# One-lane steps with 56 moving columns, and attention outputs evicted by halves

## The chip, the cores and the metric

The kernel runs on 1 core of one Trainium2 chip. The metric is the time of one execution on the device in microseconds (us). Before the change it is 3534.4 us, the median of 3 runs (3536.71, 3530.97 and 3534.40 us).

Five engines appear in the profile. PE is TensorE's stream of matmuls and PEld the weight loads in front of them, DVE is VectorE, ACT is ScalarE, POOL is GpSimd, and SP (SyncE) issues nearly all DMAs here. Matmul results land in PSUM; DVE and ACT move them on into SBUF, here called an eviction.

## The reference

Four layers stand one behind the other: a recurrent attention block A, an MLP block B, and both again with the same weights. All tensors are bf16.

```python
def _A_ref(x, mem0, Wq, Wk, Wv, Wo, seg_len):     # S 2048, Dm 640, H 32 heads, Dh 192, M 8, seg 32
    L = M + seg_len                                # 40
    mask = (idx[:, None] < M) | (idx[:, None] >= idx[None, :])
    mem = mem0
    for s in range(n_seg):                         # 64 segments, in sequence
        h = jnp.concatenate([mem, xs], axis=1)     # 40 rows: 8 of memory, 32 of the segment
        q = jnp.einsum('btd,dhe->bhte', h, Wq)     # and k, v alike
        scores = jnp.where(mask, q @ k.T * scale, -1e9)
        o = softmax(scores) @ v
        o = jnp.einsum('bhte,hed->btd', o, Wo)
        mem = o[:, :M, :]                          # the next segment's memory
        outs.append(o[:, M:, :])

x = x + _A_ref(_layernorm(x), A_mem0, ...)
x = x + _B_ref(_layernorm(x), ...)                 # layernorm, w1, gelu, shifts, w2, layernorm, w3, gelu, w4
x = x + _A_ref(_layernorm(x), A_mem0, ...)
x = x + _B_ref(_layernorm(x), ...)
```

The memory makes the 64 segments of one A a chain: a segment starts when the first 8 output rows of the one before it are there.

## The kernel before

**Steps and lanes.** The two A blocks run interleaved as two lanes. Lane 0 is the first A at segment `t`, lane 1 the second A at segment `t - LAG` with `LAG = 5`. `attention_step(t)` is called for `t` from 0 to 68. In steps 5 to 63 both lanes are there, and their rows stand side by side in one tile: the transposed input `hT` has 5 chunks of 128 partitions by `NS = 80` columns, lane 0 in columns 0 to 39 and lane 1 in 40 to 79. In steps 0 to 4 only lane 0 runs and in steps 64 to 68 only lane 1: `N` is then `L1 = 40` and `c0` (0 or 40) is the first column of the lane that runs. These ten are the one-lane steps. Every second step from t = 2 on also carries a chunk of block B (`chunk`, `chunk_end`), 64 rows of each lane; the last chunk runs alone behind step 68, the tail.

**One step.** The 32 heads go in 8 groups of 4, the groups in 4 pairs. For each pair `proj_pair` makes k, q and v, transposed: six output chunks of 128 by five contraction chunks, so 30 matmuls per group and kind, 720 in a step (L541). The weights are stationary and `hT` moves, so every matmul has a weight load of its own and moves 80 columns, or 40 in a one-lane step. q and v leave PSUM through ACT (L551, L571), k through DVE (L559, L565). v is transposed on PE (L579) and evicted in halves: ACT takes one (L590), DVE the other (L588). `attend` makes the scores (L606), the masked row minimum on DVE (L617), exp on ACT (L624), the sum and the scaling on DVE (L628 to L630), a transpose (L639) that leaves through ACT (L644), and P·V (L653). Its result `pso`, 128 partitions by 6 chunks by 80 columns in f32, leaves through one DVE cast (L659) into one of 8 buffers `oT`. The output projection takes 6 by 5 matmuls per group, 240 in a step (L670), into `psy`. All groups but the first have it due at the end of the step. `fm` (L688, ACT) then copies the 8 memory rows to the next step's `hT`, and `fy` (L696, DVE) hands the other rows to block B.

**Weights.** SBUF holds part of the weights. The rest is streamed again in every step by SP, in blocks of 384 KB through a ring of 8 buffers (L453), and block B's weights through a ring of 3 (L486 to L494). In step 0 the resident weights come in too.

**Order.** Each operation is added to a `Plan` with its engine, a length, a due time and the buffers it reads and writes. `place()` makes one list of them all by simulating the engines, the PSUM slots and the DMA rate; the program is written out in that order, so each engine works through a fixed queue. A DMA that the plan held back for its rate (`paced`) gets a wait for the PE operation that had ended by then in the plan. PSUM is 8 slots of one bank: 6 in class A, 2 in class B. Where two engines read one PSUM tile, the build puts a semaphore between them in the order in which the plan wrote them; the plan's own times do not hold that wait.

Planned lengths of matmul groups come from

```python
def mm_us(n, m=128, k=1):
    return k * (max(54, n) / 2400.0 + 0.0025)
```

Of the kernel before, what the change touches and what calls it, by code (L numbers as in the profile page):

```python
# [29 lines left out]
OT_BUFS = 8  # L30
LAT = 0.12
# [44 lines left out]
class Plan:  # L76
# [47 lines left out]
    def place(self):  # L124
# [27 lines left out]
        def est(o, t):  # L152
            s = max(t, o.ready)
            need = {}
            for b in o.slots:
                if b.slot is None:
                    need[b.cls] = need.get(b.cls, 0) + 1
            for c, n in need.items():
                fs = self.free_slots[c]
                if len(fs) < n:  # L160
                    return None
                s = max(s, fs[n - 1][0])
            if o.e == "SP":
                s = max(s, srv - ahead(o))
            return s
# [6 lines left out]
        while left:  # L172
            best = None
            for e in engines:
                t = free[e]
                lst = cand[e]
                if not lst:
                    continue
                vals = []
                m = None  # L180
                for o in lst:
                    s = est(o, t)
                    if s is not None:
                        vals.append((s, o))
                        if m is None or s < m:
                            m = s
                if m is None:
                    continue
                if best is not None and m >= best[0]:
                    continue  # L190
                lim = m + (0.12 if e == "PE" else 0.05)
                s, o = min((so for so in vals if so[0] <= lim), key=lambda so: (so[1].due, so[1].i))
                if best is None or s < best[0]:
                    best = (s, o)
            assert best is not None, "no operation can be placed"
            s, o = best
            e = o.e
            for b in o.slots:
                if b.slot is None:
                    b.slot = self.free_slots[b.cls].pop(0)[1]  # L200
            o.start = s
            o.paced = e == "SP" and s <= srv - ahead(o) + 1e-9
            o.end = s + o.d
            free[e] = o.end
            done = o.end
            if o.dma:
                srv = max(s + DMA_FIRST, srv) + o.dma / (DMA_START if o.due < STEP else DMA_RATE)
                done = srv + DMA_LAST + o.margin
            cand[e].remove(o)
            out.append(o)  # L210
            left -= 1
            for b in o.slots:
                b.left -= 1
                b.free_at = max(b.free_at, done + LAT)
                if b.left == 0:
                    heapq.heappush(self.free_slots[b.cls], (b.free_at, b.slot))
                    self.free_slots[b.cls].sort()
            for x in o.succ:
                if o.dma:
                    at = done  # L220
                elif x.e == e:
                    at = o.end
                else:
                    at = o.end + (PE_LAT if e == "PE" else LAT)
                if at > x.ready:
                    x.ready = at
                x.n -= 1
                if x.n == 0:
                    offer(x)
            if o.i in in_queue:  # L230
                q, k = in_queue[o.i]
                head[q] = k + 1
                lst = self.queues[q]
                if k + 1 < len(lst) and lst[k + 1].i in waiting:
                    x = waiting.pop(lst[k + 1].i)
                    cand[x.e].append(x)
# [4 lines left out]
def kernel(  # L241
# [87 lines left out]
    mask_b = ctile([L1, L1], bf16, "mask_b")  # L329
    nc.gpsimd.memset(mask_b[:], 0.0)  # L330
    keep(mask_b, L1, M, L1, -M, 1, -1, NEG)
    keep(mask_b, L1, M, L1, -M, 1, 0, 0.0)
# [11 lines left out]
    qT = qTw[:].rearrange("p (c n) -> p c n", c=GC)  # L344
    vFw = ctile([P, GC * NS], bf16, "vF")
    vF = vFw[:].rearrange("p (c n) -> p c n", c=GC)
    kT = [ctile([P, 8, NS], bf16, f"kT{i}") for i in range(2)]
    Vt = [ctile([NS, 2 * VP], bf16, f"V{i}") for i in range(2)]
# [23 lines left out]
    for i in range(2):  # L372
        nc.gpsimd.memset(kT[i][:], 0.0)
    for i in range(2):
        nc.vector.memset(Vt[i][:], 0.0)
    nc.gpsimd.memset(yTB[:], 0.0)
    nc.vector.memset(qTw[:], 0.0)
    nc.vector.memset(vFw[:], 0.0)
    nc.vector.memset(Pmw[:], 0.0)
# [131 lines left out]
    def attention_step(t):  # L511
# [4 lines left out]
        maskt = mask2[:] if both else (mask_a if 0 in ln else mask_b[:])  # L516
# [8 lines left out]
        def proj_pair(pr):  # L525
            s0 = base + sl * 2 * pr
            for kind, off in (("k", 0.0), ("q", 0.2), ("v", 0.5)):
                wbs, wv = load_pair(kind, pr, s0 + off * 2 * sl, LEAD_A)
                for j in range(2):
                    g = 2 * pr + j  # L530
                    G = t * NG + g
                    due = s0 + (off + 0.1 * j) * 2 * sl
# [3 lines left out]
                    for kcs in [range(0, nres)] + [range(kc, kc + 1) for kc in range(nres, KC)]:  # L536
                        def fn(op, pq=pq, wv=wv, j=j, kcs=kcs):
                            o = T(pq)
                            for cc in range(GC):
                                for kc in kcs:  # L540
                                    nc.tensor.matmul(out=o[:, cc, 0:N],  # L541
                                                     lhsT=wv(kc, GW * j + cc * P, GW * j + (cc + 1) * P),
                                                     rhs=h[:, kc, c0:c0 + N], start=(kc == 0 and cc == 0),
                                                     stop=(kc == KC - 1), skip_group_check=True)
                        wb = wbs[0] if kcs[0] == 0 else wbs[1 + kcs[0] - nres]
                        add("PE", mm_us(N, k=GC * len(kcs)), due + 0.01 * kcs[0], fn, r=(wb, *hk), a=(pq,))
                    if kind == "q":
                        q = qT

                        def fq(op, pq=pq, q=q):  # L550
                            nc.scalar.copy(out=q[:, :, 0:N], in_=T(pq)[:, :, 0:N])  # L551
                        add("ACT", act_us(GC * N), due, fq, r=(pq,), w=(B("qT"),))
                    elif kind == "k":
                        k_ = kT[G % 2]

                        def fk(op, pq=pq, k_=k_):
                            p4 = T(pq)[:].rearrange("p (h c) n -> p h c n", h=2)
                            k4 = k_[:].rearrange("p (h c) n -> p h c n", h=2)
                            nc.vector.tensor_copy(out=k4[:, :, 0::3, 0:N], in_=p4[:, :, 0::2, 0:N])  # L559
                        add("DVE", dve_us(4 * N), due, fk, r=(pq,), w=(B("kT", G % 2, 0),))  # L560
                        for part, (r0, r1, jj) in enumerate(((0, 64, 1), (64, P, 2))):
                            def fk2(op, pq=pq, k_=k_, r0=r0, r1=r1, jj=jj):
                                p4 = T(pq)[:].rearrange("p (h c) n -> p h c n", h=2)
                                k4 = k_[:].rearrange("p (h c) n -> p h c n", h=2)
                                nc.vector.tensor_copy(out=k4[r0:r1, :, jj, 0:N], in_=p4[r0:r1, :, 1, 0:N])  # L565
                            add("DVE", dve_us(2 * N), due, fk2, r=(pq,), w=(B("kT", G % 2, 1 + part),))
                    else:
                        vf, V_ = vF, Vt[G % 2]

                        def fvf(op, pq=pq, vf=vf):  # L570
                            nc.scalar.copy(out=vf[:, :, 0:N], in_=T(pq)[:, :, 0:N])  # L571
# [3 lines left out]
                        def fvt(op, pvt=pvt, vf=vf):  # L575
# [6 lines left out]
                        for hf in range(2):  # L582
                            def fe(op, pvt=pvt, V_=V_, hf=hf):
                                src = T(pvt)[0:N, GWH * hf:GWH * (hf + 1)].rearrange("n (a b) -> n a b", a=2)
                                v0 = hf * (VP - 64)
                                dst = V_[0:N, v0:v0 + 512].rearrange("n (a b) -> n a b", a=2)[:, :, 64 * hf:64 * hf + Dh]
# [5 lines left out]
                                w=(B("V", G % 2, hf),))  # L592

        def attend(g):
            G = t * NG + g
            s0 = base + sl * g
            q, k_, V_ = qT, kT[G % 2], Vt[G % 2]
# [3 lines left out]
            def fs(op):  # L601
                o = T(pss)
                seq = [(0, 1, 0, 0), (1, 1, 2, 3), (2, 1, 3, 4), (3, 1, 5, 7), (0, 2, 1, 1), (2, 2, 4, 5)]
                for n_, (i, w_, c, j) in enumerate(seq):
                    m_ = wide(c, GC - 1)
                    nc.tensor.matmul(out=o[0:m_, i * N:(i + w_) * N].rearrange("p (a b) -> p a b", a=w_),  # L606
                                     lhsT=qTw[:, c * NS:c * NS + m_], rhs=k_[:, j:j + w_, 0:N],
                                     start=(n_ == 0), stop=(n_ == len(seq) - 1), skip_group_check=True)
            add("PE", mm_us(N, N, 4) + mm_us(2 * N, N, 2), hi - 4, fs,
                r=(B("qT"), B("kT", G % 2, 0), B("kT", G % 2, 1), B("kT", G % 2, 2)), w=(pss,))  # L610
# [4 lines left out]
            def f1(op):  # L615
                o = T(pss)[0:N, 0:HG * N].rearrange("p (a b) -> p a b", a=HG)
                nc.vector.tensor_tensor_reduce(out=o, in0=o, in1=maskt.unsqueeze(1).to_broadcast([N, HG, N]),  # L617
                                               scale=-scale, scalar=3.0e38, op0=ALU.add, op1=ALU.min,
                                               accum_out=sm_[0:N, 0:1])
            add("DVE", dve_us(HG * N) + 0.02, hi - 4, f1, r=(pss,), w=(pss, smk))  # L620

            def f2(op):
                o = T(pss)[0:N, 0:HG * N].rearrange("p (a b) -> p a b", a=HG)
                nc.scalar.activation(out=Pb[0:N, :, 0:N], in_=o, func=ACT.Exp, bias=sm_[0:N, 0:1], scale=-1.0)  # L624
            add("ACT", act_us(HG * N) + 0.09, hi - 4, f2, r=(pss, smk), w=(Pk,))

            def f3(op):
                nc.vector.tensor_reduce(out=sm_[0:N, 2:2 + HG], in_=Pb[0:N, :, 0:N], axis=AX.X, op=ALU.add)  # L628
                nc.vector.reciprocal(out=sm_[0:N, 6:6 + HG], in_=sm_[0:N, 2:2 + HG])
                nc.vector.tensor_tensor(out=Pb[0:N, :, 0:N], in0=Pb[0:N, :, 0:N],  # L630
                                        in1=sm_[0:N, 6:6 + HG].unsqueeze(2).to_broadcast([N, HG, N]), op=ALU.mult)
# [11 lines left out]
            def f5(op):  # L643
                nc.scalar.copy(out=Pt[:, :, 0:N], in_=T(pst)[0:NS, :, 0:N])  # L644
# [10 lines left out]
            add("PE", mm_us(N, k=8), hi - 3, f6, r=(B("PT"), B("V", G % 2, 0), B("V", G % 2, 1)), w=(pso,))  # L655
            o_ = oT[G % OT_BUFS]

            def f7(op):
                nc.vector.tensor_copy(out=o_[:, :, 0:N], in_=T(pso)[:, :, 0:N])  # L659
            add("DVE", dve_us(GC * N), hi - 4, f7, r=(pso,), w=(B("oT", G % OT_BUFS),))  # L660
            due = base + STEP - 1 + 0.02 * g if g >= NG - OT_BUFS + 1 else s0 + 2.0 * sl
            wb, wo = res_tile(("o", g), [P, GC, Dm], Wo_v[:, g], base + STEP - 2 + 0.02 * g)
            for hf in range(2):
                def f8(op, hf=hf):
                    o = T(psy)
                    for cc in range(3 * hf, 3 * hf + 3):
                        for m in range(KC):
                            st = first_wo[0]
                            first_wo[0] = False
                            nc.tensor.matmul(out=o[:, m, c0:c0 + N], lhsT=wo[:, cc, m * P:(m + 1) * P],  # L670
                                             rhs=o_[:, cc, 0:N], start=st, stop=True, skip_group_check=True)
                add("PE", mm_us(N, k=3 * KC), due, f8, r=(wb, B("oT", G % OT_BUFS)), a=(psy,))

# [487 lines left out]
```

## Time and profile before

| what | value |
|---|---|
| median of the runs shown | 3534.4 us |
| profiled execution, own time | 3528.87 us |
| its span, first to last instruction | 3527.2 us |
| step 0 (weights come in) | 0 to 88.3 us |
| steps 1 to 4, one lane | 88.3 to 282.6 us |
| steps 5 to 63, two lanes | 282.6 to 3245.4 us |
| steps 64 to 68, one lane | 3245.4 to 3482.9 us |
| tail, the last chunk of block B | 3482.9 to 3527.2 us |
| DVE busy, ACT busy | 2469.2 us (70%), 1520.6 us (43%) |
| DMA | 1075.27 MB, mean 305 GB/s |
| mean granted TensorE clock | 0.980 |

The bounds of the steps are the ends of each step's last L670 matmuls, where `fy` starts. Busy PE time is the union of the single matmuls' spans. One matmul is in the pipeline for some 200 ns while the next starts 25 to 36 ns behind it, so a busy PE says little of its rate; that is read from the distance of starts. "issue" as releaser of a wait means that the profile shows nothing that the engine waited for.

### The profile page before, as it was taken

Reading aid. Unit: us, or ns where it says so; the run is one execution under the profiler, and the core shown is the slowest. Engines: PE = TensorE matmul, PEld = TensorE weight load, DVE = VectorE, ACT = ScalarE, POOL = GpSimd, SP = SyncE. Lnnn points to the kernel's source line nnn. Section 1 sums busy time; section 2 is a strip of 40 time slices with the busy share of each in tenths; the row PEclk is TensorE's granted clock in tenths of the full one; section 3 lists DMA queues with packets and bytes.
Section 4 is the critical chain, followed back from the end, with each engine's and each line's share of the span. In section 5 each row is a group of like instructions: output and inputs, shape, how many; then the busy total and the mean of one; then the engine's idle time right before and its main releaser. Section 6 shows DMA issues by size and latency. Waiting matters only on the chain.

```text
span 3527.2 us, 188048 instructions
## 1 busy us (share of the span) xinstructions
PE 3322.3 (94%) x84559; PEld 3231.6 (92%) x84559; DVE 2469.2 (70%) x7436; ACT 1520.6 (43%) x3569; POOL 247.1 (7%) x488
## 2 busy tenths in 40 slices
PE   5889999999999999999999999999999999999886
PEld 5879999999999999999999999999999999999775
DVE  2557777777777777777777777777777777777554
ACT  1334444444444444444444444444444444444332
POOL 0000000000000000000000000000000000000000
PEclk8899999999999999999999999999999999999897
DMA  9999898889888988898889888998889888988995
GB/s 374 304 306 317 301 324 298 294 297 316 301 307 299 315 300 299 309 321 303 302 301 327 306 295 298 316 310 303 312 305 319 298 299 301 319 300 303 307 315 176
DMA packets 497753, 1075.27 MB, mean 305 GB/s; under 512 B 49455, under 2 KB 216893, under 8 KB 496945
## 3 DMA queue, kind: packets, MB, share of 16 engines
q1 hardware_dynamic: 489712, 1050.11, 86.2%
q8 instruction: 661, 10.83, 1.2%
q0 software_dynamic: 7232, 13.13, 1.1%
q14 instruction: 148, 1.20, 0.1%
HBM read 1057.79 MB, written 5.24 MB: 301 GB/s over the span
## 4 chain that ended last, share of the span: by engine, by line
PE 88%; DMA 5%; issue 4%; DVE 1%; ACT 1%; SPq 1%; POOL 0%; POOLq 0%; DVEq 0%; ACTq 0%
PE psy L670 16%; PE psq L541 15%; PE psv L541 15%; PE psk L541 15%; PE pvt L579 5%; PE pso L653 4%; PE pss L606 4%; PE psh L998 3%; PE y L1024 3%; PE pst L639 2%; DMA wst<-in_A_Wq_dram 2%; PE psh L918 1%; DMA wst<-in_A_Wk_dram 1%; PE hs L963 1%; DMA wst<-in_A_Wv_dram 1%
## 5 line engine op out<-in xcount | busy, mean ns | idle before, releaser
L541 PEld LDWEIGHTS <-wst 128*128 128x128 bf16 x25668 | 1031.2, 100 | 43.1 <-issue 25.0
L670 PE MATMUL psy<-oT,wo 128*128 128x80 bf16 (+1 forms) x16560 | 689.8, 199 | 32.1 <-issue 19.4
L670 PEld LDWEIGHTS <-wo 128*128 128x128 bf16 x16560 | 626.3, 100 | 41.0 <-issue 29.2
L551 ACT CAST qT<-psq 128x480 bf16<-128x480 f32 (+1 forms) x552 | 292.6, 530 | 639.9 <-PE psq L541 638.6
L541 PE MATMUL psq<-hT,wst 128*128 128x80 bf16 (+1 forms) x9936 | 467.9, 199 | 19.1 <-issue 11.1
L659 DVE CAST oT<-pso 128x480 bf16<-128x480 f32 (+1 forms) x552 | 341.2, 618 | 167.2 <-PE pso L653 161.6
L541 PE MATMUL psv<-hT,wv 128*128 128x80 bf16 (+1 forms) x9936 | 434.6, 199 | 21.1 <-issue 15.9
L541 PE MATMUL psk<-hT,wst 128*128 128x80 bf16 (+1 forms) x9108 | 428.0, 199 | 11.0 <-issue 7.9
L541 PEld LDWEIGHTS <-wv 128*128 128x128 bf16 x9936 | 386.6, 100 | 28.9 <-issue 18.3
L644 ACT COPY PT<-pst 80x320 bf16<-80x320 bf16 (+1 forms) x552 | 221.9, 402 | 440.2 <-PE pst L639 433.8
L590 ACT COPY V<-pvt 80x384 bf16<-80x384 bf16 (+1 forms) x552 | 261.7, 474 | 328.5 <-PE pvt L579 301.1
L541 PE MATMUL psk<-hT,wk 128*128 128x80 bf16 (+1 forms) x7452 | 348.8, 199 | 19.5 <-ACT hT L688 10.8
L565 DVE CAST kT<-psk 64x160 bf16<-64x160 f32 (+1 forms) x1104 | 336.7, 305 | 9.7
L624 ACT ACTIVATE Pm<-pss,sm 80x320 bf16<-80x320 f32 (+1 forms) x552 | 279.7, 507 | 135.9 <-DVE sm L617 135.8
L571 ACT CAST vF<-psv 128x480 bf16<-128x480 f32 (+1 forms) x552 | 290.0, 525 | 102.0 <-PE psv L541 95.7
L541 PE MATMUL psq<-hT,wq 128*128 128x80 bf16 (+1 forms) x6624 | 320.2, 199 | 11.7 <-issue 6.6
L541 PE MATMUL psv<-hT,wst 128*128 128x80 bf16 (+1 forms) x6624 | 322.4, 199 | 7.7 <-issue 6.6
L541 PEld LDWEIGHTS <-wk 128*128 128x128 bf16 x7452 | 299.2, 100 | 26.8 <-issue 26.1
L588 DVE COPY V<-pvt 80x384 bf16<-80x384 bf16 (+1 forms) x552 | 188.1, 350 | 182.3 <-PE pvt L579 107.8
L617 DVE CUSTOM_DVE_ANT_1 pss<-pss,mask 80x320 f32<-80x320 f32 (+1 forms) x512 | 240.9, 485 | 104.7 <-PE pss L606 84.3
L559 DVE CAST kT<-psk 128x320 bf16<-128x320 f32 (+1 forms) x552 | 254.6, 461 | 69.6 <-PE psk L541 63.2
L628 DVE TENSOR_REDUCE sm<-Pm 80x4 f32<-80x320 bf16 (+1 forms) x552 | 248.9, 451 | 57.3 <-ACT Pm L624 52.2
(130 smaller groups left out, 4425.0 us busy)
## 6 DMA issues: line engine op xcount, KB each, us to landing
wst<-in_A_Wq_dram SPq DMA_DIRECT2D x828, 384.0 KB, 5.3
wst<-in_A_Wk_dram SPq DMA_DIRECT2D x759, 384.0 KB, 5.3
wst<-in_A_Wv_dram SPq DMA_DIRECT2D x552, 384.0 KB, 5.4
wstB<-in_B_w_dram SPq DMA_DIRECT2D x495, 320.0 KB, 5.0
wstB<-in_B_w_dram SPq DMA_DIRECT2D x132, 160.0 KB, 4.9
wo<-in_A_Wo_dram SPq DMA_DIRECT2D x8, 960.0 KB, 12.8
wv<-in_A_Wv_dram SPq DMA_DIRECT2D x4, 1152.0 KB, 11.9
wq<-in_A_Wq_dram SPq DMA_DIRECT2D x4, 768.0 KB, 11.7
```

The lines of the kernel that those rows point to most:

```text
L541: nc.tensor.matmul(out=o[:, cc, 0:N], lhsT=wv(kc, GW * j + cc * P, GW * j + (cc + 1) * P), rhs=h[:, kc, c0:c0 + N], start=(kc == 0 and cc ...
L551: nc.scalar.copy(out=q[:, :, 0:N], in_=T(pq)[:, :, 0:N])
L559: nc.vector.tensor_copy(out=k4[:, :, 0::3, 0:N], in_=p4[:, :, 0::2, 0:N])
L565: nc.vector.tensor_copy(out=k4[r0:r1, :, jj, 0:N], in_=p4[r0:r1, :, 1, 0:N])
L571: nc.scalar.copy(out=vf[:, :, 0:N], in_=T(pq)[:, :, 0:N])
L590: nc.scalar.copy(out=dst, in_=src)
L617: nc.vector.tensor_tensor_reduce(out=o, in0=o, in1=maskt.unsqueeze(1).to_broadcast([N, HG, N]), scale=-scale, scalar=3.0e38, op0=ALU.add, ...
L624: nc.scalar.activation(out=Pb[0:N, :, 0:N], in_=o, func=ACT.Exp, bias=sm_[0:N, 0:1], scale=-1.0)
L628: nc.vector.tensor_reduce(out=sm_[0:N, 2:2 + HG], in_=Pb[0:N, :, 0:N], axis=AX.X, op=ALU.add)
L644: nc.scalar.copy(out=Pt[:, :, 0:N], in_=T(pst)[0:NS, :, 0:N])
L659: nc.vector.tensor_copy(out=o_[:, :, 0:N], in_=T(pso)[:, :, 0:N])
L670: nc.tensor.matmul(out=o[:, m, c0:c0 + N], lhsT=wo[:, cc, m * P:(m + 1) * P], rhs=o_[:, cc, 0:N], start=st, stop=True, skip_group_check=True)
```

## The change

It has four parts.

1. **Columns.** In a one-lane step the dense projections (q, k, v) and the output projection move `W = 56` columns, of which the 40 of the running lane are kept. The window is columns 0 to 55 for lane 0 (`cw = 0`, `off = 0`) and 24 to 79 for lane 1 (`cw = 24`, `off = 16`). The evictions copy 40 columns. Tiles that only lane 1 fills keep its rows in columns 40 to 79, so that the softmax of its steps runs over 80 partitions instead of 40 (`NR`), with the same number of elements in each.
2. **Halves.** The cast of `pso` (L659) becomes two in every group of every step: chunks 0 to 2 through DVE, chunks 3 to 5 through ACT, both from the same PSUM bank. Each half has its own dependency, and the three output chunks of the projection that read it wait for that half alone.
3. **Setup.** The eight `oT` are set to zero on POOL and the four `hT` on DVE. `mask_b` is now a slice of `mask2`, and its own three small POOL operations go.
4. **Plan.** `paced` is set in `est` where the rate alone held the DMA back. New names (`KT_BUFS`, `VT_BUFS`) stand for numbers that stay as they were.

```diff
+HALVES = tuple(range(8))
+ONE = 56
...
             if o.e == "SP":
+                s0 = s
                 s = max(s, srv - ahead(o))
+                o.paced = s > s0 + 1e-9
...
-            o.paced = e == "SP" and s <= srv - ahead(o) + 1e-9
...
-    mask_b = ctile([L1, L1], bf16, "mask_b")
-    nc.gpsimd.memset(mask_b[:], 0.0)
-    keep(mask_b, L1, M, L1, -M, 1, -1, NEG)
-    keep(mask_b, L1, M, L1, -M, 1, 0, 0.0)
+    mask_b = mask2[:, L1:NS]
...
+    for o_ in oT:
+        nc.gpsimd.memset(o_[:], 0.0)
...
+    for i in range(4):
+        nc.vector.memset(hT[i][:], 0.0)
...
+        NR = c0 + N
+        W = NS if both else max(ONE, L1)
+        cw = min(c0, NS - W)
+        off = c0 - cw
...
-                                    nc.tensor.matmul(out=o[:, cc, 0:N],
+                                    nc.tensor.matmul(out=o[:, cc, 0:W],
...
-                                                     rhs=h[:, kc, c0:c0 + N], start=(kc == 0 and cc == 0),
+                                                     rhs=h[:, kc, cw:cw + W], start=(kc == 0 and cc == 0),
...
-                        add("PE", mm_us(N, k=GC * len(kcs)), due + 0.01 * kcs[0], fn, r=(wb, *hk), a=(pq,))
+                        add("PE", mm_us(W, k=GC * len(kcs)), due + 0.01 * kcs[0], fn, r=(wb, *hk), a=(pq,))
...
-                            nc.scalar.copy(out=q[:, :, 0:N], in_=T(pq)[:, :, 0:N])
+                            nc.scalar.copy(out=q[:, :, c0:c0 + N], in_=T(pq)[:, :, off:off + N])
...
-            def f7(op):
-                nc.vector.tensor_copy(out=o_[:, :, 0:N], in_=T(pso)[:, :, 0:N])
-            add("DVE", dve_us(GC * N), hi - 4, f7, r=(pso,), w=(B("oT", G % OT_BUFS),))
+            oks = [B("oT", G % OT_BUFS, hf) for hf in range(2)]
+            if g in HALVES:
+                for hf in range(2):
+                    def f7(op, hf=hf):
+                        if hf:
+                            nc.scalar.copy(out=o_[:, 3:6, off:off + N], in_=T(pso)[:, 3:6, 0:N])
+                        else:
+                            nc.vector.tensor_copy(out=o_[:, 0:3, off:off + N], in_=T(pso)[:, 0:3, 0:N])
+                    add("ACT" if hf else "DVE", (act_us if hf else dve_us)(3 * N), hi - 4, f7, r=(pso,), w=(oks[hf],))
...
-                            nc.tensor.matmul(out=o[:, m, c0:c0 + N], lhsT=wo[:, cc, m * P:(m + 1) * P],
-                                             rhs=o_[:, cc, 0:N], start=st, stop=True, skip_group_check=True)
-                add("PE", mm_us(N, k=3 * KC), due, f8, r=(wb, B("oT", G % OT_BUFS)), a=(psy,))
+                            nc.tensor.matmul(out=o[:, m, cw:cw + W], lhsT=wo[:, cc, m * P:(m + 1) * P],
+                                             rhs=o_[:, cc, 0:W], start=st, stop=True, skip_group_check=True)
+                add("PE", mm_us(W, k=3 * KC), due, f8, r=(wb, oks[hf]), a=(psy,))
```

Built, the changed program has the same 169,120 PE instructions. Its order on PE is another: cut into runs of matmuls of one kind, the program before has 6978 runs and the changed one 6889, and 5211 of them stand in the same sequence. ACT has 552 instructions more. Of the 552 pairs of halves, the build makes DVE's half wait for ACT's in 413 and ACT's wait for DVE's in 139.

## The prediction

> **What bounds the kernel now.** First the page, for what the whole span is made of.
>
> ```profile
> span 3527.2 us, 188048 instructions
> PE 3322.3 (94%) x84559; PEld 3231.6 (92%) x84559; DVE 2469.2 (70%) x7436; ACT 1520.6 (43%) x3569; POOL 247.1 (7%) x488
> PEclk8899999999999999999999999999999999999897
> q8 instruction: 661, 10.83, 1.2%
> ```
>
> PE is the busiest engine; its granted clock falls below full only at both ends. The q8 queue carries PE's own code: 169,118 matmuls and weight loads over 661 packets are 256 instructions, 128 matmuls, per 16 KB packet. The clock record shows only 1.00 and 0.50 and changes at multiples of 3.41 us. Then busy time by stage, cut at the ends of steps:
>
> ```profile
> 236.10:282.60 46.50, 41.27 (x1250) 39.52 (x1247) 32.19 (x119) 18.46 (x54) 2.57 (x6) 0.92 0.90 306
> 282.60:3245.40 2962.80, 2887.74 (x72353) 2825.08 (x72349) 2182.50 (x6359) 1345.09 (x3064) 212.86 (x411) 1.00 0.89 306
> 3292.70:3343.40 50.70, 41.52 (x1216) 38.80 (x1212) 24.85 (x95) 16.79 (x50) 4.68 (x8) 0.90 0.94 313
> ```
>
> Columns: stretch, length, busy PE, PEld, DVE, ACT, POOL, clock, DMA share, GB/s. One-lane steps last 46 to 51 us, as long as a two-lane step (2962.8 over 59 steps, 50.2), with half the columns and a clock of 0.90. To see why, matmuls in one of them by time (start, length, engine, line, tiles, form, count, wait):
>
> ```profile
> 3262.27 0.35 PE L541 MATMUL psk<-hT,wk 128*128 128x40 bf16 x8
> 3264.55 0.25 PE L541 MATMUL psk<-hT,wk 128*128 128x40 bf16 x4 [1.93 <-issue]
> 3264.66 0.74 PE L541 MATMUL psk<-hT,wst 128*128 128x40 bf16 x18
> 3265.23 0.57 PE L541 MATMUL psk<-hT,wk 128*128 128x40 bf16 x12
> ...
> 3270.18 0.46 PE L541 MATMUL psq<-hT,wq 128*128 128x40 bf16 x12
> 3270.48 0.30 PE L541 MATMUL psq<-hT,wst 128*128 128x40 bf16 x6
> ```
>
> From one start to the next: 12 matmuls in 0.30 us (25 ns) at full clock, 18 in 0.57 us (32 ns) behind the wait. The view by stretches says why: few matmuls at clock 1.00, then a stretch at half.
>
> ```profile
> 3261.30:3264.70 3.40, 1.47 (x52) 1.39 (x49) 2.47 (x11) 1.89 (x6) 0.00 (x0) 1.00 1.03 372
> 3264.70:3268.20 3.50, 3.50 (x95) 3.50 (x93) 1.41 (x5) 0.86 (x3) 0.22 (x1) 0.51 0.76 224
> ```
>
> Counting starts in order, nearly all "issue" waits in steps 64 to 68 fall at one place modulo 128, just behind a q8 packet: PE is out of code. Who waits in steps 64 to 68 (total us, times, longest):
>
> ```profile
> PEld L541 <- issue: 16.8, 15, 2.1
> PEld L670 <- issue: 7.9, 8, 2.0
> PEld L653 <- ACT V L590: 4.9, 7, 1.2
> PEld L639 <- DVE Pm L630: 2.5, 5, 0.9
> ```
>
> I cut steps 1 to 4 and 64 to 68 (428 us in whole blocks) into 84 code blocks of 128 matmuls and split each block's time: its matmuls at full clock, waits for code, other waits over 0.12 us, and the remainder, which is mostly half clock. 41 blocks end in a code wait, 50 us in all; the remainder is 24 us, and there are 24 half-clock windows. The same cut in the two-lane steps gives 2826 us of matmuls in 2942 us, 41 of code waits at the boundaries, and only some 25 us in which PE waits for ACT or DVE (an own sum over all its waits). There PE is the bound.
>
> **The change part by part.** The sum is made against the profiled execution, 3528.9 us (span 3527.2 and 1.7 around it), 5.5 below the median shown; I carry the difference over.
>
> *Columns, their price.* 56 columns are in no row. 40 move in 25 ns, 80 in 36 (in the chain of waits 30 of psq take from 1042.00 to 1043.08 us), 128 in 55 (psh L918, 15 from 3257.21 to 3258.04). The line through the last two gives 36 - 24 x 0.40 = 26.3; the floor is 25. I take 25.8, between the two and nearer the line: 0.8 ns more. Ten steps have 7200 matmuls at L541 and 2400 at L670: 9600 x 0.8 = 7.7 us, bounds 0 and 12.5. Step 0 hides its share: it moves 374 GB/s and PE waits there for DMAs. Blocks that end in a code wait hide theirs in it. At half clock the price is larger: 40 columns 33 ns (12 from 3265.23 to 3265.63), 128 some 100 (L579, 6 from 3266.23 to 3266.83), so 56 some 46 on the line between.
>
> *Columns, the clock.* [...] Each then costs 3.41 x (1 - 26/46) x 0.85 of it filled = 1.26 us, 10 in all, so 14 of 24 us go.
>
> *What is late next.* The next code packet. A block can't end before its packet; in blocks with a code wait PE goes on some 2.3 us after the packet starts. With that floor in every block, removing all half-clock time shortens the 84 blocks by 17.2 us (9.3 early, 7.9 late) with the 0.8 ns already in. For 14 of 24 that is **-10 us**. Bounds: -17 with no half clock left; +17 where every window stays at half clock and its matmuls pay 46 for 33 ns (1700 x 13 = 22, with 3 at full clock, times the 0.7 that the packets let through).
>
> [...]
>
> *Halves.* The rows, with ACT's from the q cast of the same widths:
>
> ```profile
> L659 DVE CAST oT<-pso 128x480 bf16<-128x480 f32 x472 | 308.9, 655 | 138.2 <-PE pso L653 133.0
> L659 DVE CAST oT<-pso 128x240 bf16<-128x240 f32 x80 | 32.3, 403 | 29.1 <-PE pso L653 28.6
> L551 ACT CAST qT<-psq 128x240 bf16<-128x240 f32 x80 | 28.7, 359 | 103.1 <-PE psq L541 102.0
> ```
>
> DVE falls by 472 x 0.252 + 80 x 0.126 = 129 us, ACT rises by 472 x 0.359 + 80 x 0.26 (by the slope of 480 to 240) = 190 us. But both halves read one bank, and the build orders them. The V halves show what that means: of 552 pairs (L590, L588) none overlaps, the second starts 0.03 us behind the first at best. So an eviction takes 0.36 + 0.03 + 0.40 = 0.79 us for 0.655 before, in one-lane steps 0.26 + 0.03 + 0.28 = 0.57 for 0.40. In 413 of 552 DVE stands behind ACT's half, and behind DVE's stand the softmax reduce (L628, next in its queue in 165) and V (98), for which PE waits; behind ACT's stand the q cast (137), PT (78) and V (72). The plan knows nothing of this order. Cover: the output projection is due at the end of the step, and PE waited for oT only 2.9 us in 7 cases. At the end of one-lane steps it is exposed: 0.17 x 9 = 1.5 us. In two-lane steps I take +0.5, **+2 us** together. Bounds: -8 (DVE's relief takes a third of PE's 25 us of waits) and +24 (one PT or V per step late by the other half, 0.40 x 59).
>
> [...]
>
> *Setup.* Eight POOL memsets of 128x480 at 0.58 x 480/640 = 0.44 us (kT's, 128x640, its next starts 0.58 later) less mask_b's 0.5 put 3.0 us ahead of the first L721 on POOL (7.04 us), and so of the first L541 matmul (9.43). The four hT memsets (0.9 us) sit in DVE's 3.02 us wait for POOL. PE then meets the same weights: it waits 1.0 us for wq at 12.6 and 1.8 for wv, which lands at 19.4. SP's ring waits move 3 us, with DMAs issued to 9.8 us still draining. Taken 0; +3 if uncovered.
>
> *Plan.* `paced` says the same but for ties: 0. The new PE order moves which blocks of two-lane code are dense: 0, bounds -8 and +8, a fifth of 41.
>
> Sum: -10 + 2 = -8, so 3521 for the profiled execution; from the median, **3526 us**.
>
> **Rivals.**
> *The clock comes back whole* (3526 - 7 - 6 = 3513): no half clock left (-17) and DVE's relief shows (-4). For it: the early blocks' waits for DVE. [...]
> *The packets eat it* (3535): all that PE gains it waits for code. For it: 41 of 84 blocks. Against: blocks behind a slow window end with no wait.
> *The ordered halves* (slower): 0.40 us per two-lane step, +24 - 10 + 1.5 = 3550. Its point: two-lane steps longer by over 0.14 us (8/59). For it: 413 waits of DVE on ACT, where V's already idle DVE 70.6 us in 103. Against: those cost PE only a few us.
> [...]
>
> **How the numbers follow.** 0.2% is 7 us, about what a measurement tells from no change. Forecast 0.42 (3516 to 3535: faster 0.30, same 0.12); clock whole 0.22, faster; packets 0.14 (same 0.11, faster 0.02, slower 0.01); halves 0.15 and gate 0.07, slower. Faster 0.54, same 0.23, slower 0.23. From the whole clock's 3513 less the 8 of a lucky order, 3505, to the halves' 3550: left out are about half of both slower cases (0.11) and the edge below.
>
> **What would show it.** Mean start distance of 56-column matmuls 25.8 ns; clock in steps 64 to 68 at 0.95 or more, with about half as many half-clock windows; code waits in those steps above 27 us; these steps shorter by some 5 us in all, the four early ones as much; no oT halves that overlap; two-lane steps at 50.2 ± 0.15. Wrong if one-lane steps keep their length, or two-lane steps move more than one-lane ones.

## The result, and the profile after

| kernel | median, us | executions | ratio to before, 95% |
|---|---|---|---|
| before | 3535.56 (3530.97 to 3538.52) | 6 | |
| after | 3532.66 (3524.69 to 3541.13) | 6 | 0.9992 (0.9977 to 1.0008) |
| after, timed again | 3535.20 (3523.68 to 3551.98) | 12 | 0.9996 (0.9978 to 1.0015) |

No change that can be measured. In the second timing the kernel before ran 35 times, median 3533.82, from 3519.64 to 3549.31: single executions of one program lie up to 30 us apart. So the profiled execution after, 4.2 us shorter than the one before, tells nothing by itself; what the profiles can tell is where PE's time goes.

The page after, with the lines shown of before:

```profile
span 3523.0 us, 188714 instructions
PE 3322.2 (94%) x84559; PEld 3230.5 (92%) x84559; DVE 2344.6 (67%) x7440; ACT 1696.1 (48%) x4121; POOL 250.8 (7%) x493
PEclk7999999999999999999999999999999999999998
q8 instruction: 661, 10.83, 1.2%
```

DVE lost 124.6 us and ACT gained 175.5 (forecast 129 and 190), PE's busy time is the same to 0.1 us. Busy time by stage, first after and then before, both cut at the ends of steps 0, 4, 63 and 68 (at the start of `fy`, which puts the bounds of before 0.6 us later than the table ahead of the prediction; columns as in the prediction):

```profile
88.70:281.80 193.10, 162.47 (x4850) 155.10 (x4850) 105.85 (x414) 75.73 (x230) 8.10 (x17) 0.94 0.91 308
281.80:3239.70 2957.90, 2890.78 (x72349) 2825.03 (x72347) 2066.14 (x6360) 1501.90 (x3536) 212.66 (x411) 1.00 0.89 307
3239.70:3479.00 239.30, 198.85 (x6058) 189.78 (x6057) 130.89 (x510) 93.16 (x282) 16.43 (x31) 0.97 0.90 304
```

```profile
88.90:283.20 194.30, 164.21 (x4860) 156.46 (x4860) 109.56 (x415) 67.91 (x198) 8.12 (x17) 0.89 0.91 306
3246.00:3483.50 237.50, 200.32 (x6058) 189.87 (x6057) 134.76 (x511) 83.94 (x242) 15.66 (x31) 0.91 0.91 306
```

The clock in the one-lane steps rose from 0.89 and 0.91 to 0.94 and 0.97, and yet steps 1 to 4 and 64 to 68 take 432 us together, as before. DMA share and rate didn't move either. Matmuls of one of these steps by time:

```profile
3266.84 0.47 PE L551 MATMUL psv<-hT,wst 128*128 128x56 bf16 x12
3267.15 0.60 PE L551 MATMUL psv<-hT,wv 128*128 128x56 bf16 x17
3269.12 0.19 PE L551 MATMUL psv<-hT,wv 128*128 128x56 bf16 x1 [1.38 <-issue]
3269.15 0.47 PE L551 MATMUL psv<-hT,wst 128*128 128x56 bf16 x12
3269.46 0.49 PE L589 MATMUL pvt<-ident,vF 128*128 128x128 bf16 x6
```

Twelve matmuls of 56 columns start over 0.31 us (26 ns each). One matmul short of its 18 the engine stops for lack of code, 1.38 us, and behind the stop it goes on at 26 ns: the granted clock from 3268.8 to 3272.2 us is 1.00, where before a stretch at 32 ns and a clock of 0.51 followed. Who waits in steps 64 to 68 (total us, times, longest):

```profile
DVE oT L675 <- ACT oT L673: 24.3, 22, 2.5
PEld L551 <- issue: 20.9, 20, 2.8
PEld L690 <- issue: 8.4, 11, 1.9
```

The waits for code at the dense projections were 16.8 us in 15 and are 20.9 in 20; the longest went from 2.1 to 2.8.

To add this up I split all of PE's time, from one matmul's start to the next, into the matmuls at full clock, waits over 0.12 us by what released them, and the rest, mostly half clock. A wait that the profile puts down to "issue" is counted as a wait for code: in the two-lane steps before, all 116 of them stand at the boundary of a code block. Half-clock windows are the pieces of 3.41 us that the clock record has at 0.50. This sum is used below for every kernel, in us:

| kernel | nine one-lane steps | matmuls | rest | code | ACT | DVE | half-clock windows |
|---|---|---|---|---|---|---|---|
| before | 431.7 | 318.3 | 24.8 | 51.6 | 19.0 | 17.9 | 24 |
| after | 432.5 | 323.2 | 18.3 | 54.6 | 22.3 | 14.6 | 10 |
| after, again | 433.0 | 323.2 | 14.4 | 59.6 | 22.1 | 14.2 | 8 |

| kernel | two-lane steps 5 to 63 | code | ACT | DVE | DMA |
|---|---|---|---|---|---|
| before | 2962.8 | 71.9 | 20.9 | 4.1 | 11.7 |
| after | 2957.9 | 62.8 | 24.4 | 11.9 | 5.1 |
| after, again | 2971.4 | 69.9 | 24.0 | 11.9 | 8.4 |

In the nine steps 5 us more of matmuls and 6 to 10 less of half clock stand against 3 to 8 more of code waits. In the two-lane steps the changed kernel differs by 13.5 us from one profiled execution to the other.

### The profile page after: what moved, and what is told of

The parts are those of the page before. It is cut to its first block, busy times and chain, and to the rows that moved or that the text cites. A ratio compares the mean times of both kernels' runs of the same rounds, so it can differ in the third digit from the quotient of the medians.

```text
span 3523.0 us, 188714 instructions
## 1 busy us (share of the span) xinstructions
PE 3322.2 (94%) x84559; PEld 3230.5 (92%) x84559; DVE 2344.6 (67%) x7440; ACT 1696.1 (48%) x4121; POOL 250.8 (7%) x493
## 3 DMA queue, kind: packets, MB, share of 16 engines
q8 instruction: 661, 10.83, 1.2%
## 4 chain that ended last, share of the span: by engine, by line
PE 89%; issue 4%; DMA 3%; DVE 2%; ACT 1%; SPq 1%; POOL 0%; POOLq 0%; DVEq 0%; ACTq 0%
PE psy L690 16%; PE psq L551 16%; PE psv L551 16%; PE psk L551 15%; PE pvt L589 5%; PE pso L663 4%; PE pss L616 4%; PE psh L1018 3%; PE y L1044 3%; PE pst L649 2%; PE psh L938 1%; PE hs L983 1%; DMA wst<-in_A_Wq_dram 1%; DMA wst<-in_A_Wv_dram 1%; ACT V L600 1%
## 5 line engine op out<-in xcount | busy, mean ns | idle before, releaser
L551 PE MATMUL psq<-hT,wst 128*128 128x80 bf16 (+1 forms) x9936 | 452.3, 200 | 14.3 <-issue 9.7
L675 DVE CAST oT<-pso 128x240 bf16<-128x240 f32 (+1 forms) x552 | 213.5, 387 | 314.6 <-ACT oT L673 304.8
L600 ACT COPY V<-pvt 80x384 bf16<-80x384 bf16 x552 | 262.1, 475 | 316.8 <-PE pvt L589 298.6
L551 PEld LDWEIGHTS <-wv 128*128 128x128 bf16 x9936 | 386.6, 100 | 20.5 <-issue 14.6
L634 ACT ACTIVATE Pm<-pss,sm 80x320 bf16<-80x320 f32 (+2 forms) x552 | 280.1, 507 | 140.9 <-DVE sm L627 140.9
L627 DVE CUSTOM_DVE_ANT_1 pss<-pss,mask 80x320 f32<-80x320 f32 (+2 forms) x552 | 253.7, 473 | 134.0 <-PE pss L616 120.0
L551 PE MATMUL psq<-hT,wq 128*128 128x80 bf16 (+1 forms) x6624 | 321.2, 200 | 10.3 <-DVE V L598 4.4
L598 DVE COPY V<-pvt 80x384 bf16<-80x384 bf16 x552 | 190.7, 350 | 194.4 <-ACT V L600 119.7
L673 ACT CAST oT<-pso 128x240 bf16<-128x240 f32 (+1 forms) x552 | 190.1, 344 | 267.6 <-PE pso L663 218.4
L638 DVE TENSOR_REDUCE sm<-Pm 80x4 f32<-80x320 bf16 (+2 forms) x552 | 249.4, 452 | 75.9 <-ACT Pm L634 67.0
```

The costliest lines, as they stand in the source:

```text
L551: nc.tensor.matmul(out=o[:, cc, 0:W], lhsT=wv(kc, GW * j + cc * P, GW * j + (cc + 1) * P), rhs=h[:, kc, cw:cw + W], start=(kc == 0 and cc ...
L598: nc.vector.tensor_copy(out=dst, in_=src)
L600: nc.scalar.copy(out=dst, in_=src)
L634: nc.scalar.activation(out=Pb[0:NR, :, c0:c0 + N], in_=o, func=ACT.Exp, bias=sm_[0:NR, 0:1], scale=-1.0)
L638: nc.vector.tensor_reduce(out=sm_[0:NR, 2:2 + HG], in_=Pb[0:NR, :, c0:c0 + N], axis=AX.X, op=ALU.add)
L675: nc.vector.tensor_copy(out=o_[:, 0:3, off:off + N], in_=T(pso)[:, 0:3, 0:N])
```

## The experiments

Theory: in one-lane steps PE can't be faster than its code arrives, and the code arrives behind the weight traffic; so 56 columns buy nothing there. Rivals: the columns do gain, and the halves take it back; or the columns cost what the clock gives.

**The change again, and its two halves undone, alone and together** (35 runs of before on the same chip). `e1_after_again` is the changed kernel as it is.

> The changed kernel itself, timed once more beside its variants. Both theories: 3525 to 3540 us, a ratio to the kernel before of 0.998 to 1.000, steps 1 to 4 and 64 to 68 together 432 us within 3 (431.8 before, 432.5 in the changed kernel's profile).

3535.20 us, 0.9996 (0.9978 to 1.0015): the same.

`e2_cols40` moves 40 columns again; the planned lengths keep 56, so that every queue has the order of the changed kernel.

```diff
+MOVE = 40
...
-        W = NS if both else max(ONE, L1)
+        W = NS if both else max(MOVE, L1)
+        WP = NS if both else max(ONE, L1)
...
-                        add("PE", mm_us(W, k=GC * len(kcs)), due + 0.01 * kcs[0], fn, r=(wb, *hk), a=(pq,))
+                        add("PE", mm_us(WP, k=GC * len(kcs)), due + 0.01 * kcs[0], fn, r=(wb, *hk), a=(pq,))
```

> The changed kernel with 40 moving columns in one-lane steps, planned with the length of 56, so that every queue keeps its order. Theory 'code packets' (the nine one-lane steps 1 to 4 and 64 to 68 are as long as PE's code takes to come in, so a faster clock is spent on waiting for code): the nine steps 432 us within 4, some 22 half-clock windows in them instead of 10, code waits no longer than with 56; time within 0.15% of the changed kernel. Rival 'clock' (the half-clock windows cost what they seem to, some 10 us, and something else in the change took it back): the nine steps 440 us or more and the time some 10 us (0.3%) above the changed kernel.

3536.43 us, 0.9999 (0.9981 to 1.0018). The nine steps took 426.9 us (432 within 4 expected) with 17 half-clock windows (some 22 expected) and 52.8 of code waits: no longer than with 56 columns, and `e5_own_whole` below has 426.2 with 56. The rival's 10 us are not there: what 56 columns give the clock doesn't show in the time.

`e3_whole_cast` puts the whole cast where DVE's half stands, and a copy of one column in place of ACT's half, in the same order:

```diff
-                            nc.scalar.copy(out=o_[:, 3:6, off:off + N], in_=T(pso)[:, 3:6, 0:N])
+                            nc.scalar.copy(out=spare[:, 1:2], in_=spare[:, 0:1])
-                            nc.vector.tensor_copy(out=o_[:, 0:3, off:off + N], in_=T(pso)[:, 0:3, 0:N])
+                            nc.vector.tensor_copy(out=o_[:, :, off:off + N], in_=T(pso)[:, :, 0:N])
```

> The changed kernel with the attention output leaving PSUM whole through VectorE again, in the place of its half; ScalarE copies one element of an unrelated tile in the place of the other half, so that every queue keeps its order and only the pair on one bank is gone. Theory 'no matter' (output projections are late enough): time within 0.2% of the changed kernel, two-lane steps 50.1 us on average within 0.15. Rival 'ordered halves cost' (VectorE stands behind ScalarE's half for 305 us in all and hands on the delay): two-lane steps 0.2 us shorter or more, time 10 us or more below the changed kernel. Rival 'relief' (a VectorE with 130 us more work delays the softmax): 8 us or more above it.

3546.78 us, 1.0033 (1.0014 to 1.0052): the theory by which the cast doesn't matter fails, and so does the rival that the ordered halves cost; the rival "relief" holds in this order. `e4_cols40_whole` is both edits.

> Both undone in the changed kernel's order: 40 columns and the whole cast. What is left of the change is its order of the queues and its setup. Theory: within 0.2% of the kernel before and of the changed one, and the four kernels of this series within 8 us of each other. A rival, that columns and halves each move the time by 8 us or more and cancel: then e2 and e3 lie on opposite sides of the changed kernel and this one beside it.

3544.21 us, 1.0024 (1.0007 to 1.0042): slower than before, though columns and cast are those of before. What is left is the order, with the setup and the one-column copies on ACT. The time lies where the order acts: in `e3_whole_cast` the two-lane steps took 2980.9 us, and PE waited there 24.4 us for DVE, twice as much as after, while its waits for ACT stayed at 24.9 us (24.4 after). From its waits in steps 5 to 63:

```profile
DVE oT L677 <- PE pso L665: 146.8, 127, 3.3
PE psy L692 <- DVE oT L677: 6.1, 31, 0.7
```

Where the order was made for halves, DVE's relief is worth about 12 us (3547 for 3535). The columns again make no difference: 40 and 56 give 3544 and 3547.

**The whole cast in an order of its own.** `e5_own_whole` sets `HALVES = ()`, so that the plan knows of the 480-wide cast; 56 columns stay.

> The changed kernel with the whole cast on VectorE in all groups, planned as such, so that the queues are ordered for it; 56 columns stay. Theory 'the plan had covered it' (e3 was slow because its order was planned for a VectorE with 130 us less to do): two-lane steps 2963 us within 8 as in the kernel before, PE's waits for VectorE in them 4 to 8 us instead of 24, time within 0.2% of the kernel before. Rival 'relief' (VectorE's work itself delays PE whatever the order, by the 17 us between e3 and the mean of e1 and the changed kernel): two-lane steps 2975 us or more, ratio 1.002 or more.

3530.69 us (12 executions; before 3535.20 in 22), 0.9986 (0.9968 to 1.0003), and PE's waits for DVE in two-lane steps 4.4 us, as before the change. The two-lane steps took 2969.3 us, within the 8 us expected. The plan had already laid its order around the long cast; the halves were relief for nothing.

**Where the one-lane steps' time comes from.** `e6_light` takes the traffic away: in steps 1 to 4 and 64 to 68 each streamed block brings 128 of its 1536 columns, and the projections read resident weights instead (the numbers computed there are other ones, in all else the same instructions).

```diff
+                n = 128 if few else PW
-                nc.sync.dma_start(out=T(b)[:, 0:PW], in_=w_src[kind][:, kc, cols])
+                nc.sync.dma_start(out=T(b)[:, 0:n], in_=w_src[kind][:, kc, PW * pr:PW * pr + n])
+            if few:
+                kc = kc % nres
```

> The changed kernel; in steps 1 to 4 and 64 to 68 the projections take resident weights in place of the streamed ones, of which each DMA brings only 128 of 1536 columns (so the output is not the reference's). Every queue keeps its order and PE its instructions; those steps move some 11 MB less each. Theory 'code packets behind weight traffic': the packets come sooner, code waits in the nine steps fall from 55 us to under 15, the steps from 432 us to 395 or less. Rival 'chain' (the softmax hand-overs through VectorE and ScalarE set the length): code waits fall, waits for VectorE and ScalarE take their place, the steps stay above 420. Rival 'code alone' (packets are slow by themselves): nothing changes.

One execution, 3480.56 us. Its stages 1 to 4 and 64 to 68, its two largest waits for code in steps 64 to 68, and its DMA queues there (packets, MB, share of 16 engines):

```profile
89.00:255.50 166.50, 154.36 (x4847) 148.76 (x4847) 105.41 (x414) 75.17 (x230) 8.11 (x17) 0.98 0.36 96
3230.20:3435.40 205.20, 190.43 (x6058) 183.22 (x6057) 130.21 (x511) 92.95 (x282) 16.42 (x31) 1.00 0.36 95
```

```profile
PEld L693 <- issue: 3.5, 7, 0.7
PEld L554 <- issue: 2.4, 7, 0.5
```

```profile
q1 hardware_dynamic: 32947, 18.25, 33.8%
q8 instruction: 46, 0.75, 1.6%
```

The same queues after, over the same steps:

```profile
q1 hardware_dynamic: 33292, 71.34, 87.9%
q8 instruction: 47, 0.77, 1.3%
```

The same code in almost the same number of packets, a quarter of the weights: the nine steps fall from 432 to 371.7 us, waits for code from 55 to 1.2, half-clock windows from 10 to 2. By the packet records a packet of code in steps 64 to 68 starts on average 0.84 us after PE began the block before it, against 2.23.

`e7_light40` is the same with 40 columns.

> The same with 40 moving columns. Theory: with the packets early, PE's own pace counts, half clock comes less often too (fewer code waits to trigger it), and 40 columns save their 6 us of matmuls against whatever half clock is left: nine steps within 8 us of e6. If half clock was the limit behind the packets: more half-clock windows than in e6 and steps longer by 8 us or more.

One execution, 3474.01 us; the nine steps 371.9 us, against 371.7. So even where code is no limit, 56 columns only balance: 5.3 us more of matmuls, 2.7 less of rest (7 half-clock windows become 2) and 2.3 less of code waits. As far as one execution of each can tell, both rivals on the columns fall, the gain and the loss.

`e8_cols80` is `e2_cols40` with `MOVE = 80`, which doubles what PE streams.

> The changed kernel with 80 moving columns in one-lane steps (planned with the length of 56, same order). Each of the 8640 matmuls of the nine steps takes 36 instead of 26 ns, 86 us more PE work. Theory 'code packets' (a block of 128 matmuls can't be faster than some 5 us anyway): most of it disappears in waits that end sooner; no half-clock window left, code waits from 55 to under 25 us, the nine steps 445 to 465 us, time 0.4 to 0.9% above the changed kernel. Rival 'PE paced': the nine steps 500 us or more, time 2% above.

3548.63 us (9 executions), 1.0038 (1.0022 to 1.0054). Stages 1 to 4 and 64 to 68:

```profile
88.50:286.30 197.80, 187.30 (x4850) 182.87 (x4850) 105.92 (x414) 76.28 (x231) 8.09 (x17) 1.00 0.90 301
3254.00:3501.70 247.70, 235.05 (x6058) 229.25 (x6057) 131.01 (x511) 94.24 (x282) 16.40 (x31) 1.00 0.90 294
```

Clock 1.00 throughout, 409.6 us of matmuls for 323.2, and the steps are 445.4 us for 432.5: 86 us of more work cost 13, and the 500 us of the rival "PE paced" are far off. Code waits are 2.7 us for 54.6. What PE does more it waits less. It is the other side of what `e2_cols40` shows, that the change's 10 us don't appear in the time.

**Can the code be brought sooner?** A weight DMA held back by the plan is let go when its turn at the planned rate is within `DMA_AHEAD` (1.0 us), in one-lane steps `DMA_AHEAD_ONE` (2.0). Less ahead should leave fewer weights queued in front of a packet. `e9_ahead1` sets `DMA_AHEAD_ONE = 1.0`.

> The changed kernel with DMA_AHEAD_ONE 1.0 instead of 2.0: in one-lane steps the plan lets a weight DMA go when 1 us of earlier transfers is still to come, as in two-lane steps, instead of 2 us. Theory: with a shorter row of weight DMAs in front, code packets come sooner; code waits in the nine steps from 55 to 35 us or less, the steps 10 to 20 us shorter, unless weights come late (PE's waits for DMAs, 0 us now in those steps, would then take it back). Rival: the packets wait behind whatever is in flight and the row's length is nothing: no change.

3526.26 us (10 executions; before 3536.22 in 25), 0.9978 (0.9957 to 0.9998). Its profile has 56.1 us of code waits in the nine steps and 436 us for them, so the mechanism that was expected isn't there; that profile is of its slowest execution, 3545.62. Why its median is lower stays open; the interval ends just below 1. `e10_ahead1_whole` adds `HALVES = ()`.

> The same with the whole cast planned as such. Theory: as e9; if e9 is 10 us below the changed kernel, this one is too, within 6 us of e9.

3529.04 us, 0.9985 (0.9967 to 1.0003): no difference shown, code waits in the nine steps 55.2. `e11_ahead07_whole`:

```diff
-HALVES = tuple(range(8))
+HALVES = ()
-DMA_AHEAD = 1.0
-DMA_AHEAD_ONE = 2.0
+DMA_AHEAD = 0.7
+DMA_AHEAD_ONE = 0.7
```

> The whole cast, and 0.7 us ahead in all steps but the first. Theory: code waits of two-lane steps (63 to 72 us) fall too, to 45 us or less, and PE's waits for DMAs (5 to 14 us) rise by less; time 10 to 30 us below the kernel before. Rival: the streamed weights come late, waits for DMAs rise by 20 us or more and the time with them.

3518.05 us (10 executions on the same chip), 0.9953 (0.9935 to 0.9971): the fastest version. `e10_ahead1_whole` differs from it in the 0.7 alone and ran on the same chip: 11.0 us between the medians, 10.3 between the means with a standard error of 2.7. Stages 5 to 63 and 64 to 68:

```profile
280.70:3229.10 2948.40, 2890.67 (x72339) 2825.98 (x72337) 2179.93 (x6359) 1354.30 (x3064) 209.31 (x411) 1.00 0.92 308
3229.10:3477.60 248.50, 206.41 (x6058) 195.04 (x6057) 136.30 (x510) 84.71 (x243) 15.65 (x31) 0.95 0.88 289
```

PE's waits in steps 5 to 63, after and then here:

```profile
PEld L551 <- issue: 43.9, 95, 1.3
```

```profile
PEld L551 <- issue: 18.8, 41, 0.8
PEld L649 <- DVE Pm L640: 17.9, 28, 1.4
PE psy L690 <- DVE oT L679: 13.3, 59, 0.2
```

In two-lane steps packets start 1.75 us into the block before, against 2.04 after; code waits are 17.4 us for 62.8. A part comes back as waits for DVE, 42.8 for 11.9. By this profile the gain lies in the two-lane steps; the nine one-lane steps took 440 us. The changed kernel ran on another chip, so the two compare only by their ratios to the kernel before, 0.9953 for 0.9996.

`e12_ahead07_halves` is the changed kernel with `DMA_AHEAD = 0.7` alone.

> The changed kernel, columns and halves as they are, with 0.7 us ahead in two-lane steps alone (one-lane steps keep 2.0). In e11 the two-lane code waits fell from 72 to 17 us, and PE's waits for VectorE there rose from 4 to 43 us, 23 of them for the whole cast at the end of each of the 59 steps. Theory: code waits under 30 us here too; with the halves the cast is in time, waits for VectorE in two-lane steps stay under 25 us, two-lane steps 2920 to 2950 us, one-lane steps 426 to 433 us, time 15 to 35 us below the kernel before and not above e11. Rival: the order of the halves takes as much, waits for VectorE and ScalarE together 60 us or more as in e11 (63), time as e11's or worse.

3529.89 us (12 executions; before 3535.47 in 17), 0.9985 (0.9966 to 1.0003). Code waits in two-lane steps fell here too, to 21.4 us, but the waits for DVE rose to 46.1, where under 25 were expected, and these steps took 2969.4 us for the 2920 to 2950 expected: the rival holds. From its waits in steps 5 to 63:

```profile
DVE oT L675 <- ACT oT L673: 182.2, 237, 2.7
PE psy L690 <- DVE oT L675: 26.7, 30, 0.9
```

DVE's half stands behind ACT's, and the projection behind DVE's half for up to 0.9 us, where behind the whole cast it waited 0.2 at most. In these profiles PE's waits for DVE are 11.9 us beside 62.8 of code waits (after) and 46.1 beside 21.4 (here): the ordered halves did no harm where PE was late for another reason.

## Where the prediction was right and where it was wrong

The time lies in the range, 3505 to 3550. That is no merit of the mechanism: the range is 45 us wide and holds no change at all as well as the gain. The forecast, 8 us faster, did not come; the time of the rival "the packets eat it" (3535, chance 0.14) did, though packets are only a part of the reason. Point by point:

- *The price of a column: right.* 56 columns start 26.0 ns apart at full clock (25.8 forecast), 47 at half (46), 36 at 80 columns. The nine steps hold 5 us more of matmuls.
- *The clock: right in its direction, short in its size.* 24 half-clock windows became 10 and 8 (forecast: 10 us at 1.26 each, so 8). These 8, and with them the "14 of 24", were an estimate of mine that no run shows; the runs show the counts, and a clock of 0.94 in steps 1 to 4 for 0.89. In steps 64 to 68 it is 0.97 for 0.91 (0.95 or more forecast). The rest fell by 6.5 and 10.4 us, where 14 were forecast: it is 1.8 us for each window left, and the sum had 1.26.
- *"What is late next": the step that failed.* I let each packet of code start as long after its block as in the trace before, and then counted which blocks still ended in a wait; that gave -10. The nine steps became 0.8 and 1.3 us longer. Of the 11 us between, the clock's term has 7.5 and 3.6 and the waits for code, which rose instead of staying, 3.0 and 8.0. The packets did not keep their place: in steps 64 to 68 they start on average 2.23 and 2.25 us into the block before their own in the two profiles of the changed kernel, where it was 2.01 before (2.22 and 2.28 for 2.18 in steps 1 to 4). With 40 columns in the same order (`e2_cols40`) it is 2.25 too, so it wasn't the columns that moved them; what did stays open. What they stand behind is the weights (0.84 us with a quarter of them, in `e6_light`), and a one-lane step moves nearly as much as a two-lane one: 71.34 MB on q1 in steps 64 to 68, 14.3 a step for 15.0, at a DMA share of 0.90. `e8_cols80` and `e6_light` show it from both sides: 86 us of work more cost 13, three quarters of the weight traffic less gave 61. The chance of the rival I took from 41 stalled blocks of 84, as if the others were free.
- *Waits for code in the two-lane steps: mis-sized.* The prediction counted 41 us of them at the boundaries. They are 71.9, all at the boundaries; so the bounds of the plan's term, a fifth of 41, rested on too small a sum, and `e11_ahead07_whole` found its gain there.
- *Code waits in steps 64 to 68 above 27 us: right* (31.0). *These steps shorter by 5, the early ones as much: wrong*; I had named one-lane steps that keep their length as what would prove me wrong.
- *Halves: right in what they do.* +2 was forecast; against a whole cast in its own order (0.9986) the changed kernel (0.9996) shows no difference, with an interval of 0.18% to either side on each. The two halves of one tile never overlap in 552 pairs, and the groups show the order:

```profile
L675 DVE CAST oT<-pso 128x240 bf16<-128x240 f32 (+1 forms) x552 | 213.5, 387 | 314.6 <-ACT oT L673 304.8
L673 ACT CAST oT<-pso 128x240 bf16<-128x240 f32 (+1 forms) x552 | 190.1, 344 | 267.6 <-PE pso L663 218.4
```

  DVE stands idle 304.8 us for ACT's halves, more than twice what it is spared (125). PE's waits for ACT and DVE in two-lane steps rose from 25.0 to 36.3 us, but the length of these steps differs by no more than one program's does from one execution to another. The rival "ordered halves" had the right mechanism and too high a price; `e12_ahead07_halves` shows the point at which it starts to count.
- *Setup: right.* Step 0 ends at 88.7 us, before at 88.9; the memsets are hidden. *Plan: 0, right* as far as the spread lets one see; two-lane steps are 50.1 and 50.4 us in two executions of the changed kernel, 50.2 before (50.2 within 0.15 forecast, which the second just misses).
- *0.2% as what a measurement tells* was near: with 12 and 35 executions the interval is 0.18% to either side.

What stays open: whether a packet is late because the weights issued ahead of it must drain, or because the DMA engines have too little left at a share of 0.9. `e11_ahead07_whole` speaks for the first in two-lane steps, and didn't cut code waits in steps 64 to 68 by more than some 5 us (25.9 for 31.0).

## What to carry to other kernels

Here every matmul has a weight load of its own, and PE used up 16 KB of its program per 128 matmuls (661 packets, 10.83 MB, for 84,559 matmuls). This code came late behind streamed weights, 2.23 us into the block before for 0.84 with a quarter of them: in stretches of few columns and full traffic, look at "issue" waits at code boundaries and the DMA share before giving PE faster or fuller matmuls. Less traffic helped there (371.7 us for 432.5). Fewer DMAs issued ahead helped in the two-lane steps (code waits 17.4 us for 62.8); the one-lane steps got no shorter by it (440 us for 432.5). Relief of an engine that the order already covers was worth nothing here (0.9996 with it, 0.9986 without); it got a price (12 us) only once a new order had been planned around it.

## What the hardware showed that was not expected

- Doubling the columns from 40 to 80 in 8640 matmuls of the nine steps, 91 us more of matmuls at full clock, brought their granted clock from 0.89 and 0.91 to 1.00 and cost 0.4% of the time.
- Without the weight traffic 46 code packets take 1.6% of the 16 engines' time in a 205 us stretch (52 us of engine time), with it 1.3% in 239 us (50 us): the packets themselves are not slower, they start later (2.23 us into the block before for 0.84).
- In steps 1 to 4 and 64 to 68 the clock record fell from 1.00 to 0.50 17 times before the change and 8 times after it. One of these falls, at 3264.7 us before the change, stands behind a wait of 1.93 us. What makes the clock fall was not shown.
